# A two-layer decode kernel on one core: accumulators in turn, one V moved back from PSUM two quarters later, and a slot for the dependent chain in the middle of every V scored ahead

## The chip, the cores and the metric

The kernel runs on one core of one Trainium2 chip. The metric is the device time of one execution in microseconds (us). A core has five engines with their own instruction streams: PE (TensorE, matrix multiplication), DVE (VectorE), ACT (ScalarE), POOL (GpSimd) and SP (SyncE, which here only issues DMA transfers). Each stream is worked off in order; an instruction that waits holds up everything behind it on its engine. Before the change three runs took 1104.87, 1106.29 and 1110.95 us; the median is 1106.29 us.

## The reference

For eight sequences (`b` = 0 to 7), each with one new token of 448 numbers, two layers run, each an attention over a long cache and then a small MLP. Both layers read the same caches and the same weights.

```python
def _A_ref(x, k_cache, v_cache, wq, wo):        # Hq = 16 heads of Dh = 256, Hkv = 8, Sk = 4096
    q = (x @ wq) ...                            # per head
    scores = einsum("bhqd,bhkd->bhqk", q, k) * (Dh ** -0.5)
    p = softmax(scores, axis=-1)
    o = einsum("bhqk,bhkd->bhqd", p, v)
    return o.reshape(B, Sq, Hq * Dh) @ wo

def _B_ref(x, w1, w2, w3, w4):                  # with one token per sequence the shifted parts vanish
    x1 = x + hs
    h2 = gelu(layernorm(x1) @ w3) @ w4
    return x1 + h2

x = x + _A_ref(layernorm(x), k, v, wq, wo)
x = x + _B_ref(layernorm(x), ...)
x = x + _A_ref(layernorm(x), k, v, wq, wo)      # same caches again
x = x + _B_ref(layernorm(x), ...)
```

For one sequence K and V are 16.8 MB each. What the second layer needs of a sequence (its new query) depends on everything that the first layer computed for that sequence.

## The kernel before, in words

**Units and items.** The work is cut into units `(ps, b, gp)`: layer `ps` (0 or 1), sequence `b`, and `gp` (0 to 3), a pair of the eight K/V heads. A unit has four quarters of K and four of V, 1 MB each. An item is one such quarter, `(unit, kv, c)` with `kv` 0 for K and 1 for V. The list `items` (built by `block` and `first_kept`, lines 555 to 608) is the order of all work, written out when the program is built; each engine runs its share of it in this order.

**Places.** SBUF holds 15 places of 1 MB (`places`). SP issues a transfer for the next item in `loads` when a place comes free (`emit_loads`, line 711). A K quarter is transposed in place by three DVE instructions (line 764), multiplied on PE with the query (`scores`, line 779), and goes through the exponential on ACT (`exps`, line 788). A V quarter is multiplied by the probabilities on PE in 16 matmuls (`pv`, line 832), which add into an accumulator in PSUM. The place is free again when its last reader is done. The first V quarters scored ahead (`halved`) are loaded in two halves of 512 KB, so that each half can be loaded as soon as half a place is free.

**What is kept.** The units with `gp` 2 and 3 ("kept pairs") stay for the second layer: of layer 0 of sequence `b`, twelve quarters remain in their places until layer 1 of the same `b` uses them; one V quarter (`inner`, unit `gp` 2, `c` 1) waits in PSUM instead: `away` (line 799) moves it to four PSUM banks with four DVE transposes, `back` (line 806) moves it into the place that the first kept K quarter leaves. A quarter of another V is kept in a fifth bank (lines 1064 and 1077).

**The chain.** Between the last V of layer 0 of a sequence and the first K of its layer 1 lies a chain of small dependent steps (`chain`, line 494): scale the attention result (`half`: z_cols, a copy of the accumulator to SBUF by ACT, line 467, a clear of the accumulator by DVE, line 468, two small matmuls, line 473), multiply by `wo` (line 365), normalise (`norm`, lines 227 to 302, with a power on POOL), multiply by `w3` (line 383), gelu (lines 400 to 405, its result is HT), multiply by `w4` (line 365), normalise, multiply by `wq` (line 316), and spread the query (`spread_q`, lines 335 and 339). To keep the transfers running meanwhile, `first_kept` puts V quarters of units that were scored ahead behind the kept pairs: 16 of them in the blocks that come before layer 1 of sequences 0 to 5, and 8 in the blocks for sequences 6 and 7. The first ten (`AFTER`), or all eight, come before layer 1's first K item; the rest stand between the K items of the kept pairs.

**Slots.** The steps are Python generators, advanced by `step` (line 889). A generator gives control back with `yield`. In the items named in `narrow` (the first ten V quarters scored ahead) `step` is called with `calm`, once in the middle of the V, after 8 of its 16 matmuls, and once behind it. In every other V it is called in front of it and behind it. With `calm`, a `yield 0` does not end the step, and a `yield 2` lets the next slot pass without a step. Besides the chain of the present sequence there are generators of the kind "last" (`last`, `first_last`: finish half of layer 1 of a sequence) and `first_half` (finish the first half of layer 0), which use `half` as well.

**Accumulators.** `o_banks` (line 124) are the two halves of one PSUM tile `o` of 128x512 numbers. A new group takes the first half that is not in `in_use` (line 1038); `half` gives it back once it is cleared (line 469).

Of the kernel before, what the change touches and what calls it, by code (L numbers as in the profile page):

```python
# [17 lines left out]
def kernel(  # L18
# [105 lines left out]
    o_banks = [o_both[:, 0:Dh], o_both[:, Dh : 2 * Dh]]  # L124
# [64 lines left out]
    def wblk(t, cols, c, fc):  # L189

        if fc < 3:
            return t[:, fc * cols + 128 * c : fc * cols + 128 * c + 128], fc
        half = cols // 2
        if 128 * c < half:
            return t[:, 3 * cols + 128 * c : 3 * cols + 128 * c + 128], 4
        return t[:, 3 * cols + 128 * c - half : 3 * cols + 128 * c - half + 128], 3
# [179 lines left out]
    def mlp_hidden(b0, nb):  # L376

        yield from norm(xT[:, :, b0 : b0 + nb], nb, True)
        h_ps = room_ps("h", nb)
        for c in range(HC):  # L380
            for fc in range(4):
                w, xi = wblk(w3_sb, F, c, fc)
                nc.tensor.matmul(  # L383
                    h_ps[:, c * nb : c * nb + nb],
                    w,
                    xbs(nb)[:, xi, :],
                    start=(fc == 0),
                    stop=(fc == 3),
                )
            if c % 7 == 6:  # L390
                yield 0 if c == HC - 1 else None
        g_t = chn.tile([128, 2, HC * MID], FP32, tag="g")
        hh, g0 = g_t[:, 0, 0 : HC * nb], g_t[:, 1, 0 : HC * nb]
        if nb == 1:
            HT_t = chn.tile([128, HC, 1], BF16, tag="HT")
            HT = HT_t[:]
        else:
            HT = HTw[:, :, b0 : b0 + nb]

        nc.vector.tensor_scalar_mul(hh, h_ps, 0.5)  # L400
        nc.vector.scalar_tensor_tensor(g0, hh, 2 * 0.044715, h_ps, ALU.mult, ALU.mult)
        nc.vector.scalar_tensor_tensor(g0, g0, 1.0, h_ps, ALU.add, ALU.mult)
        nc.scalar.activation(g0, g0, ACT.Tanh, scale=0.7978845608028654)
        yield 0
        nc.vector.scalar_tensor_tensor(
            HT,
            g0.rearrange("p (c b) -> p c b", b=nb),
            1.0,
            hh.rearrange("p (c b) -> p c b", b=nb),
            ALU.add,  # L410
            ALU.mult,
        )
        yield
        return HT

    def mlp(b0, nb):
# [34 lines left out]
    def half(o_ps, zall, g8, OT, ready):  # L451

        while locked:
            yield
        locked.append(g8)
        rz = yield from z_cols(zall, range(2 * g8, 2 * g8 + 2))

        R = chn.tile([128, 8], FP32, tag="R")
        nc.vector.tensor_mul(
            R[:].rearrange("p (g n) -> p g n", n=4),  # L460
            rz[:].rearrange("p n g -> p g n"),
            fold[:].rearrange("p (g n) -> p g n", n=4),
        )
        while not ready():
            yield
        o_sb = chn.tile([128, Dh], FP32, tag="o_sb")
        nc.scalar.copy(o_sb[:], o_ps)  # L467
        nc.vector.memset(o_ps, 0.0)  # L468
        in_use[:] = [t for t in in_use if t is not o_ps]
        yield  # L470
        ot_ps = ot_bank[:, 16 * g8 : 16 * g8 + 16].rearrange("p (j h) -> p j h", j=2)
        for j in range(2):
            nc.tensor.matmul(  # L473
                ot_ps[:, j], o_sb[:].rearrange("p (i j) -> p j i", j=2)[:, j], R[:], start=True, stop=True
            )
        yield 0
        nc.vector.tensor_copy(OT, ot_ps)
        locked.pop()
        yield

    locked = []
    in_use = []

    def first_half(b, st, ready):

# [54 lines left out]
    keep = sorted({gp for gp, _, _ in kept})  # L540
# [8 lines left out]
        ahead.append(units)  # L549

    tasks, items, due = [], [], []
    number, narrow, halved = {}, set(), set()
    AFTER = 10

    def block(k, v=None):
# [19 lines left out]
    def first_kept(b, units, before):  # L575

        k2, k3 = ((0, b, gp) for gp in keep)
        todo = list(units)
        block(todo.pop(0), before)
        if len(todo) > 2:  # L580
            block(todo.pop(0))
        block(k2)
        block(todo.pop(0), k2) if todo else block(None, k2)
        block(k3)
        block(todo.pop(0), k3) if todo else block(None, k3)
        assert not todo
        items.extend(due)
        due.clear()
        for u in units:
            due.extend((number[u], 1, c) for c in range(4))  # L590
        narrow.update(due[:AFTER])
        halved.update(due[: AFTER + 2])
        items.extend(due[:AFTER])
        del due[:AFTER]
# [12 lines left out]
            block((1, b, free[1]), (1, b, free[0]))  # L607
            block(None, (1, b, free[1]))
    saved = {u for units in ahead for u in units}
    calm = True  # L610

    def stays(it):
        n, kv, c = it
# [38 lines left out]
    now = [0]  # L652
# [236 lines left out]
    def step(idx, calm=False, kinds=("chain", "last", "rest")):  # L889

        for kind in kinds:
            e = next((e for e in gens if e["kind"] == kind), None)
            if e is None or (kind == "last" and alone and not e.get("locks") and idx < len(items)):
                continue
            if calm and e["skip"]:
                e["skip"] -= 1
                continue
            if not e["of"] or e["n"] < e["of"] * (idx - e["at"] + 1) / max(e["until"] - e["at"], 1):
                e["n"] += 1
                had = len(locked)  # L900
                got = next(e["g"], gens)
                while calm and got == 0:
                    got = next(e["g"], gens)
                if len(locked) != had:
                    e["locks"] = len(locked) > had
                e["skip"] = 1 if got == 2 else 0
                if got is gens:
                    gens.remove(e)
# [31 lines left out]
    for idx, it in enumerate(items):  # L940
# [7 lines left out]
        n, kv, c = it  # L948
        ps, b, gp = tasks[n]
# [8 lines left out]
        if kv == 0:  # L958
# [6 lines left out]
            st = state[ps, b]  # L965
# [30 lines left out]
            if c % 2 == 1:  # L996
                exps(p_of[n], st["z"], gp, c // 2)
                if kept_now:
                    alone.clear()
            if (ps, gp, c) == (1, keep[-1], 1):  # L1000
                where[(b, inner[0]), inner[1:]] = kept_place
                back(slots[kept_place])
        else:
            st = state[ps, b]
# [11 lines left out]
            if final and gp in free:  # L1016
                pv_cols(oc, slot, c, gp, psv[slot_of[n]])
                if c % 2 == 1:

                    u = c // 2  # L1020
                    scale_o(oc, rz_gp, gp, u, OT2[:, :, :, b])
                    h0 = 8 * gp + 4 * u
                    run(
                        add_cols(
                            st["y"],
                            lambda i: OT2[:, i % 2, i // 2, MID:],
                            wo_sb,
                            range(h0, h0 + 4),
                            4,
                            open=(claim(st), gp == free[-1] and u == 1),  # L1030
                        )
                    )
            else:
                g8 = gp // 2
                if ("o", g8) not in st:
                    while len(in_use) == 2:
                        step(10 * len(items))
                    st["o", g8] = next(t for t in o_banks if all(t is not u for u in in_use))
                    in_use.append(st["o", g8])
                if c == 0 and pairs_done.get((ps, b), 0) % 2 == 1:  # L1040
                    done = pairs_done[ps, b] + 1

                    def ready(k=(ps, b), done=done):
                        return pairs_done[k] >= done

                    if ps == 0:
                        g = (first_half if done == 2 else chain)(b, st, ready)
                        add_gen("chain", g)
                    elif done == 2:
                        add_gen("chain" if final else "last", first_last(b, st, ready))  # L1050
                    else:
                        add_gen("last", last(b, st, ready))
                pv(
                    st["o", g8],
                    slot,
                    c,
                    gp,
                    ring_of[it],
                    (lambda: step(idx, calm)) if it in narrow else None,
                )  # L1060
                if ps == 0 and inside(it):
                    away(slot)
                if ps == 0 and halfway(it):
                    nc.vector.transpose(store[4][:].bitcast(U32), slot[:, 0:Q4].bitcast(U32))
# [13 lines left out]
                slots[where[soon]][:, 0:Q4].bitcast(U32), store[4][:].bitcast(U32)  # L1078
            )
        emit_loads()  # L1080
        step(idx, it in narrow and calm)
    while gens:
        step(10 * len(items))

# [63 lines left out]
```

## Time and profile before

One execution was profiled: 1105.07 us, its span (first to last instruction) 1103.2 us. The median of the three runs is 1.2 us above it.

| engine | busy us | share of the span |
|---|---|---|
| PE | 658.1 | 60% |
| DVE | 603.5 | 55% |
| ACT | 160.6 | 15% |
| POOL | 16.3 | 1% |
| DMA, mean rate | 438.23 MB | 397 GB/s |

No engine is busy all the time, and the 16 DMA engines are busy nearly always by the page, at rates that change: about 425 GB/s in stretches in which K is loaded, less around the chain. The work repeats with a period of about 130.5 us for sequences 1 to 5 and of about 95 us for the last two; the moves of `back` that show in the chain of work start at 315.84, 446.24, 579.84, 710.40, 841.89, 948.83 and 1043.93 us (sequences 1 to 7). A table by stretch shows the rate; "chain" is the stretch with the V quarters scored ahead in front of layer 1, "kept" the one that follows it, with the kept pairs of layer 1.

| sequence | chain stretch, us | GB/s | kept stretch, us | GB/s |
|---|---|---|---|---|
| 1 | 282 to 312 | 378 | 312 to 332 | 387 |
| 2 | 412 to 442 | 390 | 442 to 462 | 387 |
| 4 | 676 to 707 | 385 | 707 to 725 | 388 |
| 5 | 808 to 838 | 382 | 838 to 856 | 387 |
| 7 | 1011 to 1042 | 355 | 1042 to 1058 | 329 |

### The profile page before, as it was taken

How to read it: one execution, taken by the hardware profiler on the slowest of the kernel's cores; microseconds unless marked ns; L12 is line 12 of the kernel's file. 1: busy time of each engine (PE TensorE's matmuls, PEld its weight loads, DVE VectorE, ACT ScalarE, POOL GpSimd, SP SyncE). 2: the span in 40 equal slices, each digit the busy share in tenths (PEclk: the TensorE clock that was granted, in tenths of full speed). 3: DMA queues.
4: the chain of work that ended last, by engine and by line, in shares of the span. 5: the costliest groups of instructions: out<-in, count | busy, mean ns of one | idle time of the engine just before them, and what ended most of it. 6: DMA issues, size and time to landing. Idle time of an engine off the chain costs nothing.

```text
span 1103.2 us, 30150 instructions
## 1 busy us (share of the span) xinstructions
PE 658.1 (60%) x13492; PEld 414.2 (38%) x13492; DVE 603.5 (55%) x1242; ACT 160.6 (15%) x610; POOL 16.3 (1%) x27
## 2 busy tenths in 40 slices
PE   3244468644776357764586445774477646766775
PEld 2122235422444225432354223442245424444555
DVE  4257742488326971278614784248832673566371
ACT  0011111111111111211102111121111111112020
POOL 0000000000000000000000000000000000000000
PEclk9999855655556555655557555575555555565565
DMA  9999999999999999999999999999999999899994
GB/s 361 395 424 427 422 389 347 427 423 421 396 372 427 424 418 389 397 425 422 402 365 393 425 427 397 389 412 425 427 384 387 424 423 409 340 426 411 341 380 197
DMA packets 67761, 438.23 MB, mean 397 GB/s; under 512 B 7208, under 2 KB 11184, under 8 KB 35504
## 3 DMA queue, kind: packets, MB, share of 16 engines
q1 hardware_dynamic: 67440, 435.94, 97.6%
q8 instruction: 105, 1.72, 0.6%
q10 hardware_dynamic: 192, 0.38, 0.1%
q14 instruction: 24, 0.20, 0.0%
HBM read 436.28 MB, written 0.01 MB: 395 GB/s over the span
## 4 chain that ended last, share of the span: by engine, by line
DMA 44%; PE 24%; DVE 22%; issue 3%; SPq 3%; ACT 2%; POOL 1%; DVEq 0%; ACTq 0%
DMA places<-in_A_k_cache_dram 23%; DMA places<-in_A_v_cache_dram 20%; DVE places L764 14%; PE sc L779 8%; PE o L832 7%; PE misc L365 3%; PE misc L316 2%; SPq L174 2%; DVE places L806 2%; PE misc L383 2%; DVE store L799 2%; PE misc L473 1%; SPq L751 1%; POOL t L254 1%; DVE qbd L339 1%
## 5 line engine op out<-in xcount | busy, mean ns | idle before, releaser
L764 DVE STREAM_TRANSPOSE places<-places 128x512 uint32<-128x512 uint32 (+1 forms) x576 | 457.0, 854 | 107.1 <-DMA places<-in_A_k_cache_dram 97.9
L779 PE MATMUL sc<-places,qbd 128*8 128x256 bf16 (+1 forms) x5120 | 253.9, 350 | 251.8 <-DVE places L764 237.7
L832 PE MATMUL o<-places,ptw 128*8 128x256 bf16 x3968 | 244.7, 384 | 109.9 <-DMA places<-in_A_v_cache_dram 81.9
L779 PEld LDWEIGHTS <-qbd 128*8 128x8 bf16 x5120 | 132.8, 105 | 330.5 <-DVE places L764 135.9
L832 PEld LDWEIGHTS <-ptw 128*8 128x8 bf16 x3968 | 99.8, 102 | 173.1 <-issue 92.7
L788 ACT ACTIVATE p_n<-sc 128x256 bf16<-128x256 f32 x128 | 95.0, 742 | 391.2 <-PE sc L779 391.2
L936 ACT COPY ptw<-psv 128x32 bf16<-128x32 bf16 x248 | 51.9, 226 | 185.0 <-PE o L832 165.8
L468 DVE MEMSET o<- 128x256 f32 x31 | 8.4, 272 | 90.7 <-ACT o_sb L467 55.7
L822 ACT CAST psv<-misc 128x128 bf16<-128x128 f32 x64 | 17.0, 266 | 266.3 <-PE misc L815 266.3
L316 PEld LDWEIGHTS <-wq_sb 128*128 128x128 bf16 x1152 | 34.8, 104 | 29.9 <-issue 19.7
L365 PEld LDWEIGHTS <-wo_sb 128*128 128x128 bf16 x1280 | 37.1, 103 | 16.2 <-issue 16.1
L806 DVE STREAM_TRANSPOSE places<-store 128x512 uint32<-128x512 uint32 x32 | 20.1, 685 | 31.8 <-PE sc L779 31.8
L316 PE MATMUL misc<-xb,wq_sb 128*128 128x1 bf16 x1024 | 33.5, 165 | 6.5 <-DVE xb L283 5.5
L473 PE MATMUL misc<-R,o_sb 128*128 128x8 f32 x124 | 28.6, 341 | 9.7 <-ACT o_sb L467 9.7
L473 PEld LDWEIGHTS misc<-R,o_sb 128*128 128x128 f32 x124 | 25.7, 288 | 21.9 <-ACT o_sb L467 18.3
L788 ACT ACTIVATION_READ_ACCUMULATOR p_n<-sc 128x1 f32 x128 | 33.6, 262 | 0.0
L365 PE MATMUL misc<-OT,wo_sb 128*128 128x1 bf16 x1024 | 31.1, 165 | 0.2 <-issue 0.2
L339 DVE CAST qbd<-misc 32x64 bf16<-32x64 f32 x92 | 19.8, 216 | 20.4 <-PE misc L335 19.5
L437 PE MATMUL misc<-zm,one 128*128 128x8 f32 (+1 forms) x66 | 17.9, 344 | 21.2 <-DVE zm L429 21.2
L254 POOL TENSOR_TENSOR t<-t,nhalf 128x2 f32<-128x2 f32 (+2 forms) x20 | 14.0, 703 | 1074.8 <-DVE t L275 1074.8
L440 DVE RECIPROCAL rz<-misc 128x8 f32<-128x8 f32 (+1 forms) x33 | 6.4, 193 | 41.5 <-PE misc L437 41.5
L437 PEld LDWEIGHTS misc<-zm,one 128*128 128x128 f32 x66 | 15.0, 282 | 33.8 <-issue 24.7
(104 smaller groups left out, 291.0 us busy)
## 6 DMA issues: line engine op xcount, KB each, us to landing
places<-in_A_k_cache_dram SPq DMA_DIRECT2D x63, 2048.0 KB, 23.8
places<-in_A_v_cache_dram SPq DMA_DIRECT2D x119, 1024.0 KB, 17.9
places<-in_A_v_cache_dram SPq DMA_DIRECT2D x178, 512.0 KB, 7.0
places<-in_A_k_cache_dram SPq DMA_DIRECT2D x66, 1024.0 KB, 14.2
places<-in_A_v_cache_dram SPq DMA_DIRECT2D x8, 768.0 KB, 8.4
wo_sb<-in_A_wo_dram SPq DMA_DIRECT2D x1, 3584.0 KB, 28.4
wq_sb<-in_A_wq_dram SPq DMA_DIRECT2D x3, 1024.0 KB, 8.0
w_sb<-in_B_w_dram SPq DMA_DIRECT2D x1, 1568.0 KB
```

What stands on the lines that cost most here:

```text
L254: nc.gpsimd.tensor_tensor(rs[:, k0:k1].rearrange("p n b -> p (n b)"), ve[:, k0:k1].rearrange("p n b -> p (n b)"), nhalf[:].to_broadcast([1 ...
L316: nc.tensor.matmul(q_ps[:, j * Hq + h, :], w, xbs(nb)[:, xi, :], start=(fc == 0), stop=(fc == 3),)
L339: nc.vector.tensor_copy(qbd[32 * a : 32 * a + 32, :, :, a, :], qs.rearrange("p e (f g u h) -> p (e f) u g h", f=2, u=2, h=2)[:, :, u],)
L365: nc.tensor.matmul(y_ps[:, fc, :], w[:, i, at : at + 128], rhs(i), start=start, stop=stop, skip_group_check=open is not None,)
L437: nc.tensor.matmul(z_ps, ones, zm[:], start=True, stop=True)
L473: nc.tensor.matmul(ot_ps[:, j], o_sb[:].rearrange("p (i j) -> p j i", j=2)[:, j], R[:], start=True, stop=True)
L764: nc.vector.transpose(w, w)
L779: nc.tensor.matmul(sc[32 * k : 32 * k + 8, 128 * x : 128 * (x + nx)], qbd[:, ep, gp].rearrange("p a h -> p (a h)"), v, start=(n == 0), sto ...
L788: nc.scalar.activation(p_sb[:, :, :, 2 * u : 2 * u + 2].rearrange("p t i x -> p x t i"), sc[:, 256 * u : 256 * u + 256].rearrange("p (x t ...
L806: nc.vector.transpose(slot[:].bitcast(U32)[:, 512 * n : 512 * n + 512], store[n][:].bitcast(U32))
L832: nc.tensor.matmul(o_ps[32 * q : 32 * q + 8, :], ptz[:, at : at + 8], v[:, y * Dh : (y + 1) * Dh], start=False, stop=(y >= 12), skip_group ...
L936: nc.scalar.copy(ptw[:, ring_of[it], :, 6:8], psv[slot_of[it[0]]][:, it[2]])
```

## The change

Five edits, which together leave the number of instructions of each kind as it was:

- `free_o` replaces `in_use`: the two accumulators are taken in turn, the one that was given back first is taken first.
- `back` is called behind the second pair of kept K quarters (`c` 3) instead of the first (`c` 1).
- `narrow` holds all V quarters scored ahead, not only the first ten: the six others now have a slot in their middle too, and none in front.
- `mlp_hidden` ends with `yield 2` behind HT: the next slot passes without a step.
- `loose` names the items of the blocks with more than eight V quarters scored ahead. Slots are only let pass there; in the blocks for sequences 6 and 7 every slot is used.

```diff
@@ mlp_hidden
-        yield
+        yield 2
         return HT
@@ half
         nc.scalar.copy(o_sb[:], o_ps)
         nc.vector.memset(o_ps, 0.0)
-        in_use[:] = [t for t in in_use if t is not o_ps]
+        free_o.append(o_ps)
@@
-    in_use = []
+    free_o = list(o_banks)
@@ first_kept
-        narrow.update(due[:AFTER])
+        narrow.update(due)
+        if len(due) > 8:
+            loose.update(due)
@@ step
-            if calm and e["skip"]:
+            if calm and e["skip"] and items[now[0]] in loose:
                 e["skip"] -= 1
                 continue
@@ the loop over the items
-            if (ps, gp, c) == (1, keep[-1], 1):
+            if (ps, gp, c) == (1, keep[-1], 3):
                 where[(b, inner[0]), inner[1:]] = kept_place
                 back(slots[kept_place])
...
-                    while len(in_use) == 2:
+                    while not free_o:
                         step(10 * len(items))
-                    st["o", g8] = next(t for t in o_banks if all(t is not u for u in in_use))
-                    in_use.append(st["o", g8])
+                    st["o", g8] = free_o.pop(0)
...
-                    (lambda: step(idx, calm)) if it in narrow else None,
+                    (lambda: step(idx, True)) if it in narrow else None,
...
-        step(idx, it in narrow and calm)
+        step(idx, it in narrow)
```

More of the change, by code (lines that the diff above doesn't have):

```diff
@@ L551 @@
     tasks, items, due = [], [], []
-    number, narrow, halved = {}, set(), set()
+    number, narrow, halved, loose = {}, set(), set(), set()
     AFTER = 10
@@ L609 @@
     saved = {u for units in ahead for u in units}
-    calm = True
     def stays(it):
```

## The prediction

> **What bounds the kernel now.** First the page's row of slices, to see whether transfers, not an engine, are the limit.
>
> ```profile
> DMA  9999999999999999999999999999999999899994
> GB/s 361 395 424 427 422 389 347 427 423 421 396 372 427 424 418 389 397 425 422 402 365 393 425 427 397 389 412 425 427 384 387 424 423 409 340 426 411 341 380 197
> ```
>
> The DMA engines hardly ever rest, but their rate dips in every period of the work. At 425 GB/s throughout, the 438.23 MB would take 1031 us of the span of 1103.2; some 70 us lie in the dips and at both ends. Then the same by stretches of sequence 3: chain, kept pairs, the K loads behind them, and the kept pairs of sequence 6 (columns: stretch, its length and busy us of PE, weight loads, DVE, ACT, POOL, then clock, DMA share, GB/s).
>
> ```profile
> 545.00:577.00 32.00, 24.00 (x508) 15.36 (x508) 5.80 (x32) 3.57 (x16) 1.26 (x2) 0.50 0.99 367
> 577.00:597.00 20.00, 13.62 (x284) 9.30 (x283) 5.33 (x17) 3.90 (x16) 0.00 (x0) 0.67 0.98 374
> 597.00:617.00 20.00, 11.62 (x286) 7.42 (x279) 13.48 (x21) 3.33 (x14) 0.00 (x0) 0.67 1.02 428
> 946.00:962.00 16.00, 10.34 (x162) 6.02 (x166) 11.15 (x23) 3.56 (x12) 0.00 (x0) 0.50 0.86 327
> ```
>
> Around the chain only three places are not taken by kept quarters, so a transfer starts when PE lets go of a place: there PE's pace sets the rate, 367 and 374 GB/s. Behind it transfers run at 428. So a us that PE loses in the first two stretches can be lost to the end, and a us saved there can be saved, up to what the transfers can take. Third, the timeline of PE in the kept stretch (start, length, what, in brackets the idle time in front and what ended it), and the DVE row beside it.
>
> ```profile
> 578.77 1.02 PE L779 MATMUL sc<-places,qbd 128*8 128x256 bf16 x16
> 582.86 0.57 PE L437 MATMUL misc<-zm,one 128*128 128x8 f32 x2 [3.06 <-DVE zm L429]
> 583.35 1.02 PE L832 MATMUL o<-places,ptw 128*8 128x256 bf16 x16
> 584.86 1.02 PE L473 MATMUL misc<-R,o_sb 128*128 128x8 f32 x4 [0.48 <-ACT o_sb L467]
> ...
> 593.87 0.61 PE L832 MATMUL o<-places,ptw 128*8 128x256 bf16 x16 [2.20 <-DMA places<-in_A_v_cache_dram]
> ```
>
> ```profile
> 579.82 2.51 DVE L806 STREAM_TRANSPOSE places<-store 128x512 uint32<-128x512 uint32 x4 [6.04 <-PE sc L779]
> 582.35 0.16 DVE L426 TENSOR_TENSOR zs_t<-z_t 128x2 f32<-128x2 f32 x1
> 582.54 0.17 DVE L429 TENSOR_TENSOR zm<-zs_t,usel 128x8 f32<-128x8 f32 x1
> ```
>
> `back` must wait for the kept scores that read its place, and zm, two tiny operations of the generator `last`, stand behind it on DVE. The next matmul in PE's order needs zm: PE stands for 3.06 us. Last, the list of waits (total us, times, longest).
>
> ```profile
> PE misc L437 <- DVE zm L429: 21.2, 7, 3.1
> PE o L832 <- DVE o L468: 7.8, 9, 0.9
> PE misc L365 <- DVE HT_t L405: 4.8, 8, 0.6
> ```
>
> The first is the case just shown, in seven blocks (five of 3.06 us, two of 2.96); the others are a V that waits for the clear of an accumulator, and the `w4` step that waits for HT.
>
> **The change part by part.** The sum is made against the profiled execution's 1105.07 us.
>
> *Back later, sequences 1 to 5.* In the changed order of DVE the zm of `last` stands in front of the four moves, and the moves need nothing that is late: the scores that read their place are five items back. So the 3.06 us go. The new slot in the middle of the V also moves: the matmul of L437, the copy (L467, 0.37 us) and the clear (L468, 0.27) come after 8 of its 16 matmuls, and the other 8 wait for the clear. Its price is the same stall as in the chain's first V, 0.87 us; in return L473 no longer waits 0.48 for the copy. PE is ahead by 3.06 + 0.48 - 0.87 = 2.67 us. Where the moves' 2.51 us go: behind the copy of line 477 and ahead of the next zm (`first_half`), which PE needs only after a V (1.02), the next kept scores (1.92) and half a V (0.60), 3.5 us at the half clock of these rows, against 2.51 + 0.16 + 0.17 = 2.84. Without that cover (at full clock the same rows are 0.61, 0.9 and 0.3, say 1.8) PE would wait 1 us. No K is transposed on DVE until 599.31 us, so the moves collide with none, and the V that they bring is used a unit later. How much of 2.67 arrives at the end: the last V of the stretch waits 2.20 us for its transfer, and at 425 GB/s the stretch's 374 leave 20 x (1 - 374/425) = 2.4 us to win (1.8 at 387). The transfer itself starts when a V two items earlier is done, so it moves too, but queues behind others. Bounds 0 and 2.67; I take 1.1, a little under half: 5.5 us in five blocks.
>
> *Back later, sequences 6 and 7.* Here 2.96 us go; no V stands between the kept scores, so no new stall; the rate is 327 and 329 GB/s, 16 x (1 - 327/425) = 3.7 us to win, and DVE starts its K transposes at 955.87, right behind this work. Bounds 0 and 2.96; I take 2.5: 5.0 us.
>
> *HT, six blocks.* The `w4` step waits 0.60 us for HT. With the slot passed, half a V (0.60 us) stands in between, and this wait goes: 3.6 us in six blocks (0 if transfers hold PE up at once). The later steps of the chain come half a V later each, the query is spread in the ninth V's middle instead of behind the eighth, still a V and a half in front of the first kept K. The places of the V's in between are let go up to one slot, 1.47 us, earlier. In sequence 3, PE ends this stretch with 2.12 and 0.67 us of waiting for V transfers; bounds 0 and 1.47, I take 0.5: 2.5 us in the five blocks where such a wait is seen.
>
> *Every slot used, sequences 6 and 7.* The two normalisations lose half a V of cover: xb is waited for 0.53 to 0.84 us now with a V (1.02) in between, and some 0.5 us longer with half of one: two in each block, 2.0 us. In return the query is ready before the first kept scores, which wait 0.99 us for it now: 2.0 us. I take 0, bounds 2 either way.
>
> *The six other V's* get the slot in their middle: what `first_half` does there is moved by half a V, and beyond the clear counted above I see no wait; 0.
>
> *Accumulators in turn.* The idea would be that a V need not wait for the clear of the half that was just given back: 0.87 us in each of eight blocks, 7.0 in all. But the trace shows the wait where the V adds into the other half: at 181.38 us the second V of a group that has its half already waits 0.82 us for the clear of a half that another group holds. In the changed order the first V behind the chain's clear still waits for DVE, for that clear. I take 0 (bounds 0 and 7.0).
>
> The Trainium skill, "PSUM — Partial Sum Buffer", section "PSUM bank collisions raise a hardware error", says to guard by bank and quadrant, not by address: two engines may not touch one bank at once even at disjoint columns. The row at 181.38 agrees; by address this edit would give 7.0 us, by bank 0.
>
> Sum: 5.5 + 5.0 + 3.6 + 2.5 = 16.6, and 1105.07 - 16.6 = 1088.5 us. The median of the runs lies 1.2 above the profiled one, so 1089.7; I say 1090.
>
> **The rivals.** *Transfers hide it.* In sequences 0 to 5 PE's lead is spent waiting for V, as the 2.20 at 593.87 and the 2.12 at the end of the chain show it can be; the page's DMA share of 0.98 to 1.00 there speaks for it, the rate of 367 to 390 against 428 speaks against. Then only the last two blocks gain, where the share is 0.86: 1106.3 - 5.0 = 1101.
>
> *The stall changes its place.* The moves now stand in front of `first_half`'s zm. If DVE starts them so late that they end after PE is there, PE waits for that: 2.84 less no cover, plus the new 0.87, against 3.06 + 0.48, is 0.2 us worse in each of five blocks, 1.0. With PE held there the HT gain is spent in front of it, and the last two blocks pay their 2.0 without the return, and their own moves hold up the copy of line 477 and the K transposes behind it by 2.5 that they gained. 1106.3 + 1.0 + 2.0 = 1109. It decides where less than 2.84 us pass between the copy of line 477 and PE's arrival at L437. The full clock from 588 on, after the stall, speaks for it; the 1.92 us of scores that ran at half clock speak against.
>
> *The accumulators do it after all:* 7 us more, 1083.
>
> **How the numbers follow.** About 0.5%, 5.5 us, is what a measurement of this kernel can tell from no change. Forecast (with the accumulators' 7 us as its better end) 0.66, transfers hide it 0.22, stall moved 0.12. The forecast's own bounds: 1106.3 less 13.4 + 5.9 + 3.6 + 7.4 + 2 is 1074, less 5.0 is 1101; all upper ends together are unlikely. The range for 8 in 10 is 1081 to 1102, which takes in the first rival and leaves out the second. Faster by over 0.5%: 0.66 and a quarter of the first rival, 0.72; within: 0.22, slower 0.06.
>
> **What would show it.** In the changed profile L437 should no longer be among PE's long waits (21.2 us now; under 4), L806's successor should start behind an L477 and not behind PE's scores, a V's second half should wait about 0.87 us for the clear in five more places, the wait for HT should fall from 4.8 to about 1.2 us, and the wait of V's for the clear should stay or grow. The kept stretches of sequences 1 to 5 should be about 1 us shorter, the last two 2.5. It is wrong if PE's waits for V transfers (81.9 us in all) grow by what L437's fall, or if a wait for zm of some 2 us is found behind the moves.

## The result, and the profile after

The changed kernel took 1092.86 us (median of 4 runs, 1090.20 to 1093.22) against 1105.58 us (4 runs of the kernel before): ratio 0.9873, 95% interval 0.9834 to 0.9912, so about 13 us or 1.3% faster. Two later comparisons of the same pair gave 0.9870 (0.9842 to 0.9899) and 0.9836 (0.9810 to 0.9863), that is 14 to 18 us. 1090 was forecast, with 1081 to 1102 as the range.

One execution was profiled: 1092.66 us, span 1090.8, which is 12.4 us less than before. First the page's row of slices of the changed kernel:

```profile
DMA  9999999999999999999999999999999999999994
GB/s 361 394 426 425 421 405 364 425 424 423 371 399 426 424 417 390 397 425 422 417 397 418 423 424 395 412 420 427 425 388 406 424 424 392 350 424 415 333 422 192
```

The same bytes at a mean of 402 GB/s instead of 397. The dips are still there (350 and 333 late in the run), most of them shallower. The stretches that the prediction showed, at their new times (chain, kept pairs, K loads of sequence 3, kept pairs of sequence 6; columns as there):

```profile
542.00:573.00 31.00, 25.38 (x540) 16.27 (x543) 6.14 (x35) 3.56 (x16) 1.25 (x2) 0.50 1.01 398
573.00:591.00 18.00, 15.00 (x311) 10.53 (x310) 4.89 (x15) 4.92 (x19) 0.00 (x0) 0.64 1.01 413
591.00:611.00 20.00, 11.61 (x255) 6.84 (x255) 14.88 (x23) 2.72 (x12) 0.00 (x0) 0.63 1.02 426
937.00:951.00 14.00, 11.77 (x187) 6.75 (x182) 11.58 (x25) 3.87 (x14) 0.00 (x0) 0.50 0.98 393
```

367, 374 and 327 GB/s have become 398, 413 and 393; behind them the rate is what it was (428 and 426). PE is busier in each of the three. In this execution the time came from where the places are let go too slowly; the part on why the prediction was right has the same stretches for all runs. Now the timeline of PE in the kept stretch of sequence 3, and DVE's beside it:

```profile
571.36 0.60 PE L833 MATMUL o<-places,ptw 128*8 128x256 bf16 x8 [0.66 <-DMA places<-in_A_v_cache_dram]
...
572.96 1.02 PE L780 MATMUL sc<-places,qbd 128*8 128x256 bf16 x16
573.78 0.64 PE L833 MATMUL o<-places,ptw 128*8 128x256 bf16 x8
574.34 0.60 PE L437 MATMUL misc<-zm,one 128*128 128x8 f32 x2
575.76 0.60 PE L833 MATMUL o<-places,ptw 128*8 128x256 bf16 x8 [0.82 <-DVE o L468]
576.29 1.02 PE L473 MATMUL misc<-R,o_sb 128*128 128x8 f32 x4
577.24 1.02 PE L833 MATMUL o<-places,ptw 128*8 128x256 bf16 x16
578.05 1.92 PE L780 MATMUL sc<-places,qbd 128*8 128x128 bf16 x64
579.76 1.06 PE L833 MATMUL o<-places,ptw 128*8 128x256 bf16 x16
580.76 0.60 PE L437 MATMUL misc<-zm,one 128*128 128x8 f32 x2
582.01 1.02 PE L833 MATMUL o<-places,ptw 128*8 128x256 bf16 x16 [0.66 <-DMA places<-in_A_v_cache_dram]
...
586.96 0.61 PE L833 MATMUL o<-places,ptw 128*8 128x256 bf16 x16 [1.05 <-DMA places<-in_A_v_cache_dram]
```

```profile
577.35 0.23 DVE L477 CAST qT<-misc 128x16 bf16<-128x16 f32 x1 [1.64 <-PE misc L473]
577.44 2.50 DVE L807 STREAM_TRANSPOSE places<-store 128x512 uint32<-128x512 uint32 x4
579.87 0.12 DVE L426 TENSOR_TENSOR zs_t<-z_t 128x2 f32<-128x2 f32 x1
580.01 0.17 DVE L429 TENSOR_TENSOR zm<-zs_t,usel 128x8 f32<-128x8 f32 x1
```

L437 follows half a V without a bracket: its wait of 3.06 us is gone. The new one of 0.82 us for the clear stands in the V's middle. The four moves run behind the copy of L477, and the next zm is ready at 580.18, 0.58 us before PE comes to it at 580.76. In the four other blocks of sequences 1 to 5 the time to spare is 0.35 to 0.58 us, and in other executions with `back` later it goes down to nearly nothing (0.05 in p1_back_and_ht): the cover that the prediction put at 3.5 us against 2.84 is there, but thin. At the top, the last V before the kept scores waits 0.66 us for its transfer where its two halves had waited 2.12 and 0.67. At the end of the stretch the last V waits 1.05 us instead of 2.20, and a V in front of it, which did not wait before, now waits 0.66. The list of waits of the changed kernel (total us, times, longest):

```profile
PE o L833 <- DMA places<-in_A_v_cache_dram: 89.7, 62, 6.0
...
PE o L833 <- DVE o L468: 11.9, 14, 0.9
...
PE misc L365 <- DVE HT_t L405: 1.7, 5, 0.6
```

The wait of L437 for zm, 21.2 us before, is no longer among PE's waits here; in the two later profiles of the same kernel 0.9 and 1.5 us of it are left, at most 0.8 in one place and none of it behind the moves. Waiting for the clear went from 9 places to 14, waiting for HT from 4.8 us to 1.7, and waiting for V transfers from 81.9 to 89.7: of 21.2 + 3.1 = 24.3 us that PE no longer waits, 4.1 came back as waiting for the clear and 7.8 as waiting for transfers.

### The profile page after: what moved, and what is told of

It reads as the page before. It is cut to its first block, busy times and chain, and to the rows that moved or that the text cites. A ratio compares the mean times of both kernels' runs of the same rounds, so it can differ in the third digit from the quotient of the medians.

```text
span 1090.8 us, 30150 instructions
## 1 busy us (share of the span) xinstructions
PE 664.3 (61%) x13492; PEld 417.0 (38%) x13492; DVE 602.8 (55%) x1242; ACT 161.9 (15%) x610; POOL 16.3 (1%) x27
## 4 chain that ended last, share of the span: by engine, by line
DMA 49%; PE 23%; DVE 19%; SPq 3%; issue 3%; ACT 2%; POOL 1%; DVEq 0%; ACTq 0%
DMA places<-in_A_k_cache_dram 25%; DMA places<-in_A_v_cache_dram 24%; DVE places L765 13%; PE sc L780 8%; PE o L833 6%; PE misc L365 3%; SPq L174 2%; DVE store L800 2%; PE misc L473 1%; PE misc L383 1%; PE misc L316 1%; ACT p_n L789 1%; SPq L752 1%; POOL t L254 1%; DVE qbd L339 1%
## 5 line engine op out<-in xcount | busy, mean ns | idle before, releaser
L780 PE MATMUL sc<-places,qbd 128*8 128x256 bf16 (+1 forms) x5120 | 257.2, 354 | 249.1 <-DVE places L765 236.4
L833 PE MATMUL o<-places,ptw 128*8 128x256 bf16 x3968 | 250.2, 389 | 120.3 <-DMA places<-in_A_v_cache_dram 89.7
L833 PEld LDWEIGHTS <-ptw 128*8 128x8 bf16 x3968 | 102.0, 103 | 186.5 <-issue 109.6
L316 PEld LDWEIGHTS <-wq_sb 128*128 128x128 bf16 x1152 | 34.5, 104 | 28.1 <-issue 17.9
L316 PE MATMUL misc<-xb,wq_sb 128*128 128x1 bf16 x1024 | 33.2, 166 | 4.7 <-DVE xb L283 3.6
L473 PEld LDWEIGHTS misc<-R,o_sb 128*128 128x128 f32 x124 | 25.1, 281 | 19.3 <-ACT o_sb L467 13.4
L473 PE MATMUL misc<-R,o_sb 128*128 128x8 f32 x124 | 28.0, 335 | 7.1 <-ACT o_sb L467 7.1
L339 DVE CAST qbd<-misc 32x64 bf16<-32x64 f32 x92 | 19.8, 216 | 20.2 <-PE misc L335 19.3
L383 PEld LDWEIGHTS <-w_sb 128*128 128x128 bf16 x560 | 17.8, 105 | 15.9 <-issue 14.9
L383 PE MATMUL misc<-xb,w_sb 128*128 128x1 bf16 (+1 forms) x560 | 18.9, 166 | 8.0 <-DVE xb L283 5.6
## 6 DMA issues: line engine op xcount, KB each, us to landing
places<-in_A_k_cache_dram SPq DMA_DIRECT2D x63, 2048.0 KB, 24.3
places<-in_A_v_cache_dram SPq DMA_DIRECT2D x119, 1024.0 KB, 18.7
```

Source lines behind the costliest of these rows:

```text
L316: nc.tensor.matmul(q_ps[:, j * Hq + h, :], w, xbs(nb)[:, xi, :], start=(fc == 0), stop=(fc == 3),)
L339: nc.vector.tensor_copy(qbd[32 * a : 32 * a + 32, :, :, a, :], qs.rearrange("p e (f g u h) -> p (e f) u g h", f=2, u=2, h=2)[:, :, u],)
L383: nc.tensor.matmul(h_ps[:, c * nb : c * nb + nb], w, xbs(nb)[:, xi, :], start=(fc == 0), stop=(fc == 3),)
L473: nc.tensor.matmul(ot_ps[:, j], o_sb[:].rearrange("p (i j) -> p j i", j=2)[:, j], R[:], start=True, stop=True)
L780: nc.tensor.matmul(sc[32 * k : 32 * k + 8, 128 * x : 128 * (x + nx)], qbd[:, ep, gp].rearrange("p a h -> p (a h)"), v, start=(n == 0), sto ...
L833: nc.tensor.matmul(o_ps[32 * q : 32 * q + 8, :], ptz[:, at : at + 8], v[:, y * Dh : (y + 1) * Dh], start=False, stop=(y >= 12), skip_group ...
```

## The experiments

All comparisons are ratios to runs of the kernel before on the same chip; the last column is the ratio's distance from 1 times 1106.3, the median that the forecast started from, with a minus where the run is faster. Where an edit is said to be alone it was made in the kernel before, where it is undone, in the changed kernel.

| run | edits in it | ratio | 95% interval | us |
|---|---|---|---|---|
| changed kernel, first | all | 0.9873 | 0.9834 to 0.9912 | -14.1 |
| n1_after_again | all | 0.9870 | 0.9842 to 0.9899 | -14.4 |
| p4_after_third | all | 0.9836 | 0.9810 to 0.9863 | -18.1 |
| e1_back_only | back | 0.9919 | 0.9889 to 0.9948 | -9.0 |
| e2_turn_only | accumulators in turn | 1.0003 | 0.9983 to 1.0023 | +0.3 |
| p2_ht_only | yield 2 behind HT | 0.9921 | 0.9895 to 0.9948 | -8.7 |
| p3_slots_only | six more middle slots | 1.0016 | 0.9996 to 1.0036 | +1.8 |
| p1_back_and_ht | back, yield 2 | 0.9831 | 0.9805 to 0.9858 | -18.7 |
| e3_undo_back | all but back | 0.9950 | 0.9931 to 0.9969 | -5.5 |
| n2_undo_ht | all but yield 2 | 0.9920 | 0.9894 to 0.9947 | -8.9 |
| e5_undo_slots | all but the slots | 0.9843 | 0.9815 to 0.9870 | -17.4 |
| n3_pass_all | all, slots passed in every block | 0.9845 | 0.9818 to 0.9872 | -17.1 |
| n4_back_twice | none, moves made twice | 1.0080 | 1.0048 to 1.0112 | +8.9 |

**The step of back, alone and undone.**

```diff
-            if (ps, gp, c) == (1, keep[-1], 1):
+            if (ps, gp, c) == (1, keep[-1], 3):
```

> The kernel before with one edit: back() behind the second kept pair. My account: the 3.06 us wait of L437 for zm goes in five blocks and the 2.96 in two; since the V's keep their slots, no V waits for a clear in its middle, so waits of V's for the clear stay near 7.8 us in 9 places. Of the changed kernel's 12.7 us this edit alone gives 8 to 11 (about 1096). Rival 'the stall changes its place': L437 still waits, under 2 us gained. Rival 'the slots do it': 2 to 4 us gained.

Measured: 0.9919, 9.0 us gained (5.8 to 12.3 by the interval). L437's wait is 0.6 us in one place, waits for the clear stay at 6.9 us in 8. This is inside the 8 to 11 of my account, and it rules out both rivals: the stall did not change its place, and the slots are not needed for it.

The changed kernel with the same line put back to 1:

> The changed kernel with back() behind the first kept pair again. My account: the gain of back is lost, 8 to 11 us, so 1101 to 1104; what is left against the kernel before (2 to 5 us) is HT, the slots and the places let go earlier. The slot in the middle of the V now stands in the same V as the wait: L437 waits for zm less, about 2.5 us instead of 3.06, since half a V is in front of it. Rival 'the slots do it': within 3 us of the changed kernel.

Measured: median 1103.65 us, 0.9950, so 8 to 9 us of the changed kernel's gain are lost beside its first two comparisons, and more beside the third. L437 waits 19.7 us in 8 places, the longest 3.0: the half V in front of it shortens the five waits of 3.06 us by 0.42 each, less than the 0.5 that I had put.

**The accumulators, alone.**

```diff
-        in_use[:] = [t for t in in_use if t is not o_ps]
+        free_o.append(o_ps)
...
-                    st["o", g8] = next(t for t in o_banks if all(t is not u for u in in_use))
-                    in_use.append(st["o", g8])
+                    st["o", g8] = free_o.pop(0)
```

> The kernel before with one edit: accumulators taken in turn. My account: the V behind the clear still waits for it, whichever half it adds into; 0 us, between 1 gained and 1 lost, and 9 waits of 0.87 us for the clear stay. Rival: the waits go and 5 to 7 us are gained.

Measured: 1.0003. The list of waits of this kernel:

```profile
PE o L832 <- DVE o L468: 7.8, 9, 0.9
```

It is the line of the kernel before, to the digit. By the order of the two programs, eight of the nine V's added into the half just cleared before, and the one at 181.38 us into the other half; taken in turn, all nine add into the other half, and they wait as long. The edit gains nothing in this kernel.

**The slots of the six other V's, undone and alone.**

```diff
-        narrow.update(due)
+        narrow.update(due[:AFTER])
```

> The changed kernel with middle slots only in the first ten V's scored ahead, as before; the six others have a slot in front and behind. My account: five waits of 0.87 us for the clear go from the middle of a V, and L473 waits 0.48 again; PE some 0.4 us better in five blocks: 0 to 2 us faster than the changed kernel, 1091 to 1093. Rival 'the slots do it': 3 us or more slower than the changed kernel.

Measured: 0.9843, median 1091.98 us. The waits for the clear are back at 7.8 us in 9 places. The changed kernel in its own comparisons, none of them beside this run, had 0.9836 to 0.9873; the difference, between 3 us faster and 1 us slower, is not resolved. The rival's 3 us or more slower is not seen.

> The kernel before with a middle slot in all V's scored ahead, alone. My account: the wait for zm moves behind half a V (2.5 instead of 3.06), a clear in a V's middle costs 0.87 in five blocks, L473's 0.48 go: within 3 us of the kernel before, either way. Rival 'the slots do it': 3 to 6 us faster.

Measured: 1.0016 (0.9996 to 1.0036), within 3 us and if anything slower. Waiting for the clear rises to 11.9 us in 14 places (4.1 more); L437 waits 19.1 us (2.1 less) and L473 7.3 instead of 9.7 us (2.4 less): what one wait gains the two others lose.

**HT, undone and alone.**

```diff
-        yield 2
+        yield
         return HT
```

> The changed kernel with a plain yield behind HT, so the slot after HT is used again. My account: HT is waited for 0.60 us in six more blocks and the places of the V's behind it are let go a slot later: 3 to 6 us slower than the changed kernel. Rival 'transfers hide it': within 1 us of the changed kernel, with less waiting of V's for transfers.

Measured: 0.9920 beside 0.9870 for the changed kernel on the same chip, 5.5 us slower, within the 3 to 6 expected. HT is waited for 4.8 us again instead of 1.7.

> The kernel before with yield 2 behind HT alone. My account: 4 to 6 us faster than the kernel before, the wait for HT near 0, L437 still waiting 21 us. In sequences 6 and 7 three passed slots do not fit into sixteen, so the first kept scores wait for the query a little longer than 0.99 us. Rival 'it needs the other edits': within 2 us of the kernel before.

Measured: 0.9921, 8.7 us gained, with runs that spread from 1095.73 to 1106.59. HT is waited for 0.7 us, L437 still 22.4; the wait for the query in sequences 6 and 7 stays at 2.0 us for both. The gain is larger than expected; its interval begins at 5.8. A second wait fell with the one for HT, that of the `wq` step (L316) for xb, the normalised vector that it multiplies; in the kernel before, then in this one:

```profile
PE misc L316 <- DVE xb L283: 5.5, 8, 0.7
```

```profile
PE misc L316 <- DVE xb L283: 2.6, 7, 0.5
```

Together the two waits fell by 4.1 + 2.9 = 7.0 us of the 8.7 gained. With HT undone (n2_undo_ht beside n1_after_again) they rise by 3.1 + 2.3 = 5.4 us of the 5.5 lost. PE's waits for V transfers did not fall with HT: 81.9 us before, 85.6 with HT alone.

**Passing slots in every block.**

```diff
-            if calm and e["skip"] and items[now[0]] in loose:
+            if calm and e["skip"]:
```

> The changed kernel with slots passed in the blocks of sequences 6 and 7 too. My account: the waits for xb there fall by about 0.5 us each, four in all, and the first kept scores wait for the query again: three passed slots leave the chain longer than the sixteen slots of eight V's, so the last steps run one behind the other in front of the scores. 0 to 4 us slower than the changed kernel. Rival: passing is good there too, 1 to 2 us faster.

Measured: 0.9845 beside 0.9870. The wait for the query came back (2.0 us in the last two blocks) and the waits for xb there fell from 4.8 to 3.1 us, so both effects exist and nearly cancel; my side of the bet, 0 to 4 us slower, is not seen, and 0 to 3 us faster is within the intervals.

**The suspected wait doubled.** In the kernel before, the moves are made twice:

```diff
                 back(slots[kept_place])
+                back(slots[kept_place])
```

> The kernel before with the four moves of back() made twice in a row, the second time with the same data: DVE reaches zm 2.5 us later, so L437 waits about 5.6 us instead of 3.06 in five blocks and 5.5 in the last two, 17.5 us more in all. It measures what share of a PE wait in this place reaches the end. My account (a little under half in the five, nearly all in the last two): 8 to 13 us slower than the kernel before. Rival 'transfers hide it': 5 us or less. If every us counts: 17 us.

Measured: 1.0080 (1.0048 to 1.0112), 8.9 us slower (5.3 to 12.4 by the interval, so the rival's 5 us or less is out by little). The stretches of this kernel (kept pairs of sequence 3, then of sequence 6) and its L437:

```profile
580.00:600.00 20.00, 12.80 (x282) 9.19 (x275) 7.73 (x21) 4.40 (x18) 0.00 (x0) 0.65 0.91 358
952.00:970.00 18.00, 10.17 (x158) 5.90 (x162) 13.17 (x26) 3.56 (x12) 0.00 (x0) 0.50 0.74 280
```

```profile
586.03 0.57 PE L437 MATMUL misc<-zm,one 128*128 128x8 f32 x2 [5.45 <-DVE zm L429]
```

Waiting for zm went from 21.2 to 38.6 us, and 8.9 of these 17.4 us, half, reached the end. The rates are 358 and 280 GB/s; with the wait as it was they were 374 and 327, in the changed kernel 413 and 393. More wait, less transfer, in both directions.

**The two edits together, and the changed kernel beside them.**

> The kernel before with two edits alone: back() behind the second kept pair, and yield 2 behind HT, with slots passed in all blocks. If the accumulators, the six other slots and the list loose bring nothing, this is at least as fast as the changed kernel: 1089 to 1093, 0 to 3 us faster than it. Rival 'the slots do part of it': 2 us or more slower than the changed kernel.

Measured: 0.9831 (0.9805 to 0.9858), median 1090.30 us, beside 0.9836 and 1090.61 for the changed kernel:

> The changed kernel once more, on the same chip as the three beside it: 1090 to 1094 us, ratio to the kernel before near 0.987.

As far as can be resolved, two lines of the change are all of its gain, and the gains of the two alone (9.0 and 8.7, on two chips) add up to the 18.7 of both within the intervals. No version was found that is faster than the changed kernel beyond doubt. The earlier repeat of the changed kernel stood beside n2_undo_ht, n3_pass_all and n4_back_twice:

> The changed kernel itself, on the same chip as the runs beside it: 1091 to 1094, the ratio 0.987 again.

It took 1094.11 us, 0.9870.

## Why the prediction was right, point by point

The sum was 16.6 us; the three comparisons of the changed kernel gave 14.1, 14.4 and 18.1.

*What bounds the kernel.* Confirmed, and for each edit in its own stretch. The table has means over sequences 1 to 5, one profiled execution of each run. The chain stretch goes from the last clear of an accumulator in front of HT to the first kept score, the kept stretch from there to the move of line 1077, the period from one such move to the next; rates are read over these stretches as above. The period of the kernel before is 131.0 us by these marks, not the 130.5 given ahead of the prediction.

| edits in it | runs | chain us | chain GB/s | kept us | kept GB/s | period us |
|---|---|---|---|---|---|---|
| neither | before, e2, p3 | 27.1 to 27.5 | 369 to 378 | 18.2 to 18.9 | 374 to 387 | 131.0 to 132.2 |
| back | e1, n2 | 26.2 to 27.2 | 374 to 376 | 17.8 to 18.1 | 406 to 408 | 130.7 to 130.8 |
| yield 2 | p2, e3 | 26.2 to 26.4 | 391 to 394 | 18.5 to 18.7 | 366 to 382 | 131.0 to 131.3 |
| both | changed kernel (3), p1, e5, n3 | 25.8 to 26.3 | 391 to 397 | 17.0 to 17.8 | 404 to 413 | 129.2 to 130.0 |
| moves twice | n4 | 26.7 | 382 | 19.8 | 354 | 132.1 |

The rate in what is left of the period is 418 to 421 GB/s in every run. So `back` raises the rate in the kept stretch and the passed slot that in the chain, and neither clearly moves the other's; only the length of the chain stretch in n2 (26.2) lies where the runs with the passed slot lie.

*Back, sequences 1 to 5* (3.06 and 0.48 go, 0.87 comes, 5.5 us of 13.4 arrive) *and 6 and 7* (5.0 of 5.9). The sum of both, 10.5 us, measured 9.0 alone and 8 to 9 by undoing. The shares can be read from the kept stretches. In sequences 1 to 5 they are 18.55 us in the mean of the five runs without the edit and 17.47 in the eight with it, 1.08 shorter where 1.1 was taken; with the moves made twice they are about 1.2 longer for 2.4 put in. In sequences 6 and 7 they are 8.33 us in each run without the edit, 5.68 with it (5.37 once) and 10.72 with the moves made twice: 2.65 of 2.96 taken out and 2.39 of 2.4 put in arrive, where 2.5 was taken. The periods are too coarse for such a reading: those of sequences 1 to 5 average 131.0 us in one execution of the kernel before and 132.2 in e2_turn_only, whose edit gains nothing. The new stall came where it was put, 0.82 us in the middle of the V, in five more places (9 to 14). In the cover for the moves two errors cancel: PE comes to L437 behind a whole V (the row at 579.76), not half of one, and rows that follow each other overlap by some 0.2 us, so the 3.5 us that the row lengths gave are 3.5 from 577.24 to 580.76 too.

*HT.* The term was 3.6 for the wait and 2.5 for places let go a slot earlier, 6.1 us; measured 5.5 undone and 8.7 alone. The first part held: the wait for HT fell from 4.8 to 1.7 us (1.2 was forecast). The second was right in size and not by its reason. It should have shown as less waiting for V transfers between HT and the first kept score, and in sequence 3 that fell, from 2.79 to 0.66 us; but in sequence 5 it rose from 2.00 to 3.32, and over sequences 1 to 5 it is 8.3 us before, 8.1 with HT alone and 7.4 in the changed kernel. What fell instead is the wait of the `wq` step for xb: in the chains of sequences 1 to 5 it is 3.2 to 3.5 us in each run without the passed slot and 0.9 to 1.9 in each with it, some 2 us that the prediction did not have. That this came to nearly the 2.5 of the other term is luck.

*Every slot used in sequences 6 and 7.* Put at 0 with 2 us either way: the wait for the query went (2.0 us), the waits for xb in these two blocks rose from 2.8 to 4.8 us, 2.0 as forecast, and n3_pass_all shows no more than 3 us between the two ways.

*The six other V's and the accumulators.* Both put at 0; measured +1.8 (interval -0.4 to 4.0) and +0.3 (interval -1.9 to 2.5). For the accumulators the step was that the row at 181.38 us already showed a wait across the halves; the unchanged 7.8 us in 9 places, with all nine now across the halves, is the proof. The end at 7.0 us of that bound can be struck out.

*Rivals.* "Transfers hide it" has a part in it: waits for V transfers rose by 7.8 us. It was not the whole, since the periods of sequences 1 to 5 became shorter too, 129.2 to 130.0 us with both edits against 131.0 to 132.2 with neither. The DMA share that spoke for it was no guide: 0.99 at 367 GB/s in the chain stretch before and 1.01 at 398 after. "The stall changes its place" did not come, with 0.58 us to spare at the place shown and 0.05 at the least in any profile.

What I had not seen: in the profiled execution the span behind the last move of line 1077 is 54.8 us, 1.9 more than the 52.9 before. It is about as long in the other runs that have both `back` later and `loose` (54.5 to 54.8), 53.9 and 53.5 in n3_pass_all and p1_back_and_ht, where slots are passed in every block, and 52.9 and 53.0 in e1_back_only and e3_undo_back. Part of it seems to go with `loose`; its cause was not tried.

## What to carry to other kernels

Where transfers wait for places, look for the instruction that stands at the head of the wait on the compute engine, and ask what stands in front of its producer in that engine's fixed order; here two 0.17 us operations stood behind 2.5 us of moves that nobody needed for a long time, and moving the moves was worth 9 us. A slot left empty behind a long dependent step is not lost: here the independent work that filled it covered the wait for that step, and a step further down the chain waited less too. When a change has five parts, run each alone: three of these five did nothing that could be measured.

## What the runs showed of the hardware

The wait of a V for the clear held to the digit when the halves of the PSUM tile were taken in turn (7.8 us, 9 places, before and in e2_turn_only): in this kernel the tile is waited for as a whole, whichever half is written. The wait is for a semaphore of the program, so it shows how the program guards the tile; what the chip would do without it no run shows.

PE at 25.38 us of 31 busy in the chain stretch (82%) was granted the half clock, 0.50, throughout. In the kept stretch behind it, with 15.00 of 18 us (83%), it was granted 0.50 up to about 586 us and 1.00 from there on, 0.64 in the mean. In the kernel before, PE shows no idle time above 0.05 us for 11.1 us from 181.4 on, at 0.50. In these stretches the busy time that the profile counts does not tell which clock is granted.
